# Attention after a GeGLU gate on one core: when the tiles of a burst are finished, and when the last output weights are loaded

## The chip, the cores and the metric

The kernel runs on one core of one Trainium2 chip. Its time is the device time of one execution in microseconds; the figure for a kernel is the median over its runs. The engines are named as in the profile: PE (TensorE) for matmuls and PEld for its weight loads, DVE (VectorE), ACT (ScalarE), POOL (GpSimd), SP (SyncE). POOL and SP issue transfers here; an issue takes its place in the queue of the engine that issues it.

## The reference

All arrays are bf16. `x` is 2048 x 448, 16 query heads share 8 heads of keys and values, a head has 256 columns, and the last 512 cached keys are attended.

```python
xn = _layernorm(x)
q = (xn @ wq)                       # 448 x 4096, 16 heads
scores = einsum("bhqd,bhkd->bhqk", q, k[last 512]) * 256 ** -0.5
s = (softmax(scores) @ v) @ wo      # wo is 4096 x 448
g = _silu((_gelu(xn @ w_gate) * (xn @ w_up)) @ w_down)
return x + s * g
```

## The kernel before

The 2048 rows are 16 tiles of 128, in 4 chunks of 512. First comes the feed-forward part over all chunks; it writes the gate `g` to `g_all` in DRAM. Then comes attention: 64 steps `m` (`NS`, loop at L895), 16 heads for each chunk. A step issues `s_mm(m)` (L712): for each of four tiles two score matmuls into a bank of the set AB, an exponential on ACT into `p` (three slots, L720), and for each pair of tiles one reciprocal and two scalings on DVE into `pn` (three slots of a pair each, L724, L727) and one DMA transpose `pT<-pn` on SP. Then the step issues `pv(m - 2)` (L733): eight matmuls of `va` with `pT` into two banks of the set BB, which ACT and DVE evacuate into `oTh` (`oT` in the last chunk). The lag of two steps is `LAG`.

The queries `qT` are made ahead of the heads, in groups (`groups`, L346): a query group at m = 18, 34, 50 makes eight heads, in four calls of `q_group` (L694) of two heads each, and so do those at 26 and 42; the one at 58 makes six. A call runs matmuls of `xnT` with `wq` and evacuates four banks: three on ACT and one on DVE (L707) where `end` is true, two and two elsewhere.

The first three chunks are not multiplied by `wo` in the plain way. At m = 17, 33, 49 `burst` (L798) multiplies `oTh` and sums of it by prepared weights `wt` and `w3` and leaves the chunk's projection transposed, in four blocks of rows. These are transposed back by DMA transposes on SP: `sN` early in the burst, three `sT` near its end. Then `burst_end(c, t4)` (L874) finishes one of the chunk's four tiles: three DVE multiplications of `sT` and `sN` with the gate tile `g` into `tmpb`, and in `wo_end` (L756) one addition onto the row tile `xr`. `wo_end` also issues three transfers on POOL: the load of the gate tile two tiles ahead (`g` has two slots), the store of the finished tile to `out`, and the load of the row tile three tiles ahead (`xr` has three slots), which must wait until the store has read the slot. "The first, second and third end" are the ends of chunks 0, 1 and 2, in the query groups at m = 18, 34 and 50 (`end`, L898).

The last chunk is multiplied by `wo` itself after the 64 steps (L930 to L944). The tile `wo` lies where `wt` and `w3` lay, so it can be loaded once the third burst's products have read those. Before, its four quarters of 896 KB are issued on POOL right after the third burst's call (L922 to L926), ahead of the query group at m = 50.

All engines run their instructions in the order of these calls. `Plan` (L43) derives the waits: an instruction waits by semaphore for those whose data or slots it needs, and an engine stands still until the wait is over. A call of `dma` on POOL is no exception: a waiting load holds the issues behind it.

Of the kernel before, what the change touches and what calls it, by code (L numbers as in the profile page):

```python
# [12 lines left out]
P = 128  # L13
# [155 lines left out]
def bass_recurrent_scan__sliding_block_cached__geglu_ffn__prompt_kernel(  # L169
# [15 lines left out]
    Hq = HD // Dh  # L185
# [7 lines left out]
    NCO = HD // P  # L193
# [17 lines left out]
    with es:  # L211
# [3 lines left out]
        def place(name, shape, dt, at=None):  # L215
            size = {BF16: 2, F16: 2, F32: 4}[dt]
            for n in shape[1:]:
                size *= n
            size = (size + 31) // 32 * 32
            if at is None:  # L220
                at = base[0]
                base[0] += size
            assert at + size <= nc.sbuf_usable_end, (name, at + size, nc.sbuf_usable_end)
            return nc.alloc_sbuf_tensor_at(name, list(shape), dt, offset=at), at, at + size

        def sbuf_bufs(at, size, n):
            return [K.buf(at + i * size, size) for i in range(n)]
# [56 lines left out]
        wo, _, _ = place("wo", [P, NCO, D], BF16, at=rw)  # L284
        b_wo = sbuf_bufs(rw, 8 * D * 2, NCO // 8)
# [67 lines left out]
        def dma(q, o, i, reads=(), writes=()):  # L353
            K.op(q, lambda e, o=o, i=i: e.dma_start(o, i), reads, writes, dma=True)  # L354
# [4 lines left out]
        def act(o, i, func, reads, writes, scale=1.0):  # L359
            K.op("act", lambda e, o=o, i=i: e.activation(o, i, func, scale=scale), reads, writes)  # L360

        def add(eng, o, x, y, reads, writes, op=ALU.add):
            K.op(eng, lambda e: e.tensor_tensor(o, x, y, op), reads, writes)  # L363

        def mms(lst, reads, writes, after=()):
            def fn(e):
                ins = None
                for (o, l, r, st, sp) in lst:
                    ins = e.matmul(o, lhsT=l, rhs=r, start=st, stop=sp, skip_group_check=True)  # L369
                return ins  # L370
            return K.op("pe", fn, reads, writes, after=after)
# [156 lines left out]
        def bk(pairs, j):  # L528
            return pairs[j // 2] + j % 2
# [8 lines left out]
        def down(c, pairs):  # L538
            for t4 in range(4):
                t = c * 4 + t4  # L540
                b = bk(pairs, t4)
                mms([(bank[b][:, 0:D], actT[:, c % 2, f, t4 * P:(t4 + 1) * P], wd[:, f, :], f == 0, f == NF - 1)
                     for f in range(NF)], [b_wd] + b_actT[c % 2], (b_ps[b],))
                s = t % 2
                act(tmp[:, s, 0:D], bank[b][:, 0:D], ACT.Tanh, (b_ps[b],), b_tmp[s], scale=0.5)
                K.op("dve", lambda e, t=t, b=b, s=s: e.scalar_tensor_tensor(
                    out=g2w[:, t % 4, :], in0=tmp[:, s, 0:D], scalar=1.0, in1=bank[b][:, 0:D],
                    op0=ALU.add, op1=ALU.mult), b_tmp[s] + [b_ps[b]], (b_g2w[t % 4],))
                dma("sp", g2d[t], g2w[:, t % 4, :], (b_g2w[t % 4],), (b_g2d[t],))
# [144 lines left out]
        def q_group(n, pairs, more_act=False):  # L694

            c, h = divmod(n, Hq)
            units = [(b, lambda j, k, i=i: wq[:, k, (h + i) * Dh + j * P:(h + i) * Dh + (j + 1) * P],
                      wqr[:, h + i, :], slice(c * QC, (c + 1) * QC), b_wql[h // HG][:1], b_wql[h // HG][1:], b_xnT[c * 4:c * 4 + 4])
                     for i, b in enumerate(pairs)]
            group(units, 0, QC, True, True)  # L700
            for i, b in enumerate(pairs):
                s = qs(n + i)
                act(qT[:, s, 0, :], bank[b], ACT.Copy, (b_ps[b],), (b_qT[s][0],))
                if more_act and i:
                    act(qT[:, s, 1, :], bank[b + 1], ACT.Copy, (b_ps[b + 1],), (b_qT[s][1],))
                    continue
                K.op("dve", lambda v, s=s, b=b: v.tensor_copy(qT[:, s, 1, :], bank[b + 1]),  # L707
                     (b_ps[b + 1],), (b_qT[s][1],))
# [24 lines left out]
        def pv(m):  # L733
            h = m % Hq
            g, x = h // 2, m % NPT
            for e in range(2):
                b = BB[m % 2 * 2 + e]
                mms([(bank[b].rearrange("p (t q) -> p t q", q=P), va[:, g, j, e * P:(e + 1) * P],
                      pT[:, x, :, :, j, :].rearrange("p a t q -> p (a t) q"), j == 0, j == NJ - 1)
                     for j in range(NJ)], [b_va[g]] + b_pT[x], (b_ps[b],))  # L740
                i = 2 * h + e
                o, f = (oTh, WS) if m < NS - Hq else (oT, 1.0)
                if e == 0:
                    act(o[:, i, :], bank[b], ACT.Copy, (b_ps[b],), (b_oT[i],), scale=f)
                else:
                    K.op("dve", lambda v, i=i, b=b, o=o, f=f: v.tensor_scalar(  # L746
                        o[:, i, :], bank[b], f, None, op0=ALU.mult), (b_ps[b],), (b_oT[i],))
# [8 lines left out]
        def wo_end(t, c0, c1, mult, bt, y):  # L756

            x, g = t % NXR, t % NG2
            bx = [b_xr[x][i] for i in range(2) if (c0 < CUT, c1 > CUT)[i]]
            mult(g2[:, g, :], b_g2[g])  # L760
            if t + NG2 < NT and c1 == D:
                load_g2(t + NG2)
            add("dve", xr[:, x, c0:c1], y[:, c0:c1], xr[:, x, c0:c1], bt + bx, bx)
            dma("sp" if t >= NT - 4 else "pool", out_view[:, t, c0:c1], xr[:, x, c0:c1], bx, ())
            if t + NXR < NT and c1 == D:
                dma("pool", xr[:, x, :], x_view[:, t + NXR, :], (), b_xr[x])
# [107 lines left out]
        def burst_end(c, t4):  # L874
            t = c * 4 + t4
            s, u = t % 2, t4 // 2
            y = tmpb[:, s, 0:D]

            def mult(g, bg):
                two = lambda x, lo, hi: x[:, 0:2 * N2].rearrange("p (n d) -> p n d", n=2)[:, :, lo:hi]  # L880
                for at, i, reads in ((lambda x: two(x, 0, P), sT[:, t4, 0:2, :], b_sT[:2]),
                                     (lambda x: two(x, P, N2), sT[:, t4, 2, :].rearrange("p (n d) -> p n d", n=2), b_sT[2:]),
                                     (lambda x: x[:, 2 * N2:D], sN[:, t4 % 2, u * R:u * R + R], [b_sN])):
                    add("dve", at(y), i, at(g), reads + [bg], b_tmp[s], ALU.mult)
            wo_end(t, 0, D, mult, b_tmp[s], y)

        LAG = 2
        late = []
        NS = NQC * Hq

        act(tmp[:, 1, 0:1], nhalf[:, :], ACT.Exp, (b_nhalf,), (b_tmp[1][0],))
# [2 lines left out]
        BB.extend(bk(nxt, j) for j in range(4))  # L894
        for m in range(NS):  # L895
            if m in groups:
                for i in range(m, groups[groups.index(m) + 1], 2):
                    end = m > Hq and m % Hq == LAG  # L898
                    q_group(i, (cur, nxt)[((i - m) // 2 + (m == Q0 + QS)) % 2], end)
                    for t4 in {4: (0, 1), 6: (2, 3)}.get(i - m, ()) if end else ():  # L900
                        burst_end(m // Hq - 1, t4)
                if m == 0:
                    K.reuse([b for x in b_pT for b in x] + b_pn + b_p32)
            if m > Hq and m % Hq == LAG:
                K.reuse(b_pn + b_p32)
            s_mm(m)
            if m < LAG:
                down(NQC - LAG + m, nxt)
                if m == LAG - 1:
                    K.reuse(b_oT + [b for y in b_qT[:QS - Q0] for b in y])  # L910
                    assert not CASTS and not SUMS
                    K.reuse(b_sT + [b_sN])
                    for t in range(NG2):
                        load_g2(t)
            if len(late) == LAG:
                pv(late.pop(0))
            if m > Hq and m % Hq == LAG - 1:
                if m // Hq == 1:
                    for b in b_xs:
                        b.old.extend(y for t in range(4) for z in b_xnT[t] for y in z.readers + [z.writer])  # L920
                burst(m // Hq - 1)
                if m // Hq == NQC - 1:  # L922
                    K.reuse(b_wo)
                    for i in range(NCO // 8):
                        dma("pool", wo[:, i * 8:(i + 1) * 8, :],
                            A_wo.rearrange("(c p) d -> p c d", p=P)[:, i * 8:(i + 1) * 8, :], (), (b_wo[i],))  # L926
            late.append(m)
        c = NQC - 1
        LATE = NCO - 2 * (LAG + 1)
# [70 lines left out]
```

The softmax here doesn't subtract the row's maximum and nothing guards it: scores larger than these inputs give would overflow.

## Time and profile before

| what | value |
|---|---|
| runs | 569.97, 562.45, 565.86, 563.88 us |
| median of the four | 564.87 us |
| profiled execution | 569.97 us, of it the span of the profile 568.2 us |
| mean granted clock of PE | 0.988 |
| PE busy | 549.0 us, 97% of the span |
| burst of chunk 0, 1, 2 ends, query group begins | 244.07, 353.36, 457.98 us |
| query group ends, heads begin | 256.50, 365.78, 470.41 us |
| issue of wo's quarters | 451.15, 458.36, 459.24, 460.11 us; to landing 5.9, 7.6, 10.5, 12.2 us |

The page is one execution. Its first section gives each engine's busy time, its second the span in slices, the fourth the chain that ended last, the fifth groups of instructions with what ended the idle time before them. Beside it the trace can be asked for the busy time in any stretch, for the instructions in order of time, and for the transfers. In a timeline line stand the start, the time, the engine, the line of the code, the operation, the tiles written and read, the shape and how many alike; in square brackets the idle time of the engine before it and what ended that. Matmuls have the line of a helper, L369, additions and multiplications of two tensors L363, plain ACT copies L360 and plain transfers L354.

### The profile page before, as it was taken

Reading aid. Unit: us, or ns where it says so; the run is one execution under the profiler, and the core shown is the slowest. Engines: PE = TensorE matmul, PEld = TensorE weight load, DVE = VectorE, ACT = ScalarE, POOL = GpSimd, SP = SyncE. Lnnn points to the kernel's source line nnn. Section 1 sums busy time; section 2 is a strip of 40 time slices with the busy share of each in tenths; the row PEclk is TensorE's granted clock in tenths of the full one; section 3 lists DMA queues with packets and bytes.
Section 4 is the critical chain, followed back from the end, with each engine's and each line's share of the span. In section 5 each row is a group of like instructions: output and inputs, shape, how many; then the busy total and the mean of one; then the engine's idle time right before and its main releaser. Section 6 shows DMA issues by size and latency. Waiting matters only on the chain.

```text
span 568.2 us, 11445 instructions
## 1 busy us (share of the span) xinstructions
PE 549.0 (97%) x4419; PEld 289.0 (51%) x4444; DVE 346.9 (61%) x804; ACT 309.9 (55%) x783; POOL 44.1 (8%) x83
## 2 busy tenths in 40 slices
PE   9999999999999999998799999989999995999997
PEld 5554444445444446953344489434446952444455
DVE  6664645753557668746565795377478734675722
ACT  5334446653568576057566831677586054776700
POOL 1141500000000000003000000120000013100000
PEclk9999999999999999999799999999999999899999
DMA  9665499712316548027642840387087174972711
GB/s 292 131 184 120 103 299 265 113 46 78 92 38 148 112 87 137 8 33 129 150 112 55 150 99 10 60 178 158 20 149 150 40 183 148 164 155 57 144 24 58
DMA packets 177766, 66.46 MB, mean 117 GB/s; under 512 B 159856, under 2 KB 173680, under 8 KB 177712
## 3 DMA queue, kind: packets, MB, share of 16 engines
q1 hardware_dynamic: 172960, 52.76, 44.2%
q0 software_dynamic: 3984, 12.39, 8.1%
q8 instruction: 35, 0.57, 0.5%
q10 hardware_dynamic: 768, 0.57, 0.3%
q14 instruction: 19, 0.16, 0.1%
HBM read 23.43 MB, written 3.67 MB: 48 GB/s over the span
## 4 chain that ended last, share of the span: by engine, by line
PE 81%; DMA 9%; DVE 5%; ACT 3%; issue 2%; POOL 1%; ACTq 0%; DVEq 0%
PE bank L369 80%; DMA pT<-pn 4%; DVE pn L727 3%; ACT p L720 3%; DMA sT<-xnT 2%; DMA g<-g_all 1%; DMA out_dram<-xr 1%; PE bank L486 1%; DVE rden L724 1%; DVE tmpb L363 0%; DVE oTh L746 0%; POOL g L354 0%; POOL xr L354 0%; DVE xr L363 0%; ACT qT L360 0%
## 5 line engine op out<-in xcount | busy, mean ns | idle before, releaser
L720 ACT ACTIVATE p<-bank 128x512 f32<-128x512 f32 x256 | 150.6, 596 | 43.3 <-DVE pn L727 32.9
L369 PE MATMUL bank<-pT,va 128*128 128x512 bf16 x512 | 124.5, 387 | 5.6 <-DMA pT<-pn 3.5
L369 PE MATMUL bank<-kT,qT 128*128 128x512 bf16 x487 | 120.9, 385 | 9.0 <-ACT p L720 6.7
L727 DVE TENSOR_SCALAR pn<-p,rden 128x512 bf16<-128x512 f32 x256 | 113.2, 485 | 12.0 <-DMA pT<-pn 7.7
L369 PE MATMUL bank<-xnT,wq 64*128 64x512 bf16 x768 | 94.9, 376 | 0.5 <-DVE oTh L746 0.5
L369 PEld LDWEIGHTS bank<-kT,qT 128*128 128x128 bf16 x512 | 49.8, 99 | 71.7 <-ACT p L720 8.4
L369 PEld LDWEIGHTS bank<-pT,va 128*128 128x128 bf16 x512 | 50.2, 99 | 70.0 <-DMA pT<-pn 7.0
L369 PE MATMUL bank<-xnT,wgu 64*128 64x512 bf16 (+2 forms) x768 | 83.9, 350 | 0.1
L360 ACT ACTIVATE qT<-bank 128x512 bf16<-128x512 f32 x76 | 44.1, 596 | 54.1 <-PE bank L369 52.5
L707 DVE CAST qT<-bank 128x512 bf16<-128x512 f32 x52 | 35.1, 692 | 46.9 <-PE bank L369 46.8
L369 PEld LDWEIGHTS bank<-xnT,wq 64*128 64x128 bf16 x768 | 36.6, 94 | 47.1 <-ACT p L720 1.7
L369 PEld LDWEIGHTS bank<-xnT,wgu 64*128 64x128 bf16 x768 | 37.0, 94 | 36.9 <-issue 0.7
L535 DVE TENSOR_TENSOR actT<-bank,gl 128x512 bf16<-128x512 f32 x56 | 37.8, 690 | 26.5 <-PE bank L369 19.9
L360 ACT ACTIVATE gl<-bank 128x512 bf16<-128x512 f32 x56 | 33.2, 597 | 37.1 <-PE bank L369 34.9
L720 ACT ACTIVATION_READ_ACCUMULATOR p<-bank 128x1 f32 x256 | 51.4, 201 | 0.0
L724 DVE RECIPROCAL rden<-rsum 128x2 f32<-128x2 f32 x128 | 21.2, 165 | 47.3 <-ACT p L720 47.2
L369 PE MATMUL bank<-wd,actT 128*128 128x448 bf16 x224 | 43.0, 353 | 0.0
L354 POOL DMA_DIRECT2D g<-g_all x16 | 8.8, 549 | 351.8 <-DVE tmpb L363 287.6
L746 DVE TENSOR_SCALAR oTh<-bank 128x512 f16<-128x512 f32 x48 | 32.8, 684 | 0.8 <-PE bank L369 0.8
L369 PEld LDWEIGHTS bank<-wd,actT 128*128 128x128 bf16 x224 | 21.8, 98 | 21.0 <-DVE mv L419 0.4
L369 PE MATMUL bank<-sr,wt 128*64 128x256 f16 x576 | 31.9, 273 | 0.0
L369 PEld LDWEIGHTS bank<-sr,wt 128*64 128x64 f16 x576 | 31.5, 110 | 0.0
(63 smaller groups left out, 415.3 us busy)
## 6 DMA issues: line engine op xcount, KB each, us to landing
wo<-in_A_wo_dram POOLq DMA_DIRECT2D x4, 896.0 KB, 9.0
wtb<-in_A_wo_dram POOLq DMA_DIRECT2D x4, 768.0 KB, 7.4
wq<-in_A_wq_dram SPq DMA_DIRECT2D x2, 1536.0 KB, 8.3
va<-in_A_v_cache_dram SPq DMA_DIRECT2D x8, 256.0 KB, 6.1
pT<-pn SPq DMA_TRANSPOSE x128, 2.8
g_all<-g2w SPq DMA_DIRECT2D x16, 112.0 KB, 2.1
xr<-in_A_x_dram POOLq DMA_DIRECT2D x16, 112.0 KB, 2.6
g<-g_all POOLq DMA_DIRECT2D x16, 112.0 KB, 2.5
```

Source lines behind the costliest of these rows:

```text
L354: K.op(q, lambda e, o=o, i=i: e.dma_start(o, i), reads, writes, dma=True)
L360: K.op("act", lambda e, o=o, i=i: e.activation(o, i, func, scale=scale), reads, writes)
L369: ins = e.matmul(o, lhsT=l, rhs=r, start=st, stop=sp, skip_group_check=True)
L486: ins = e.matmul(bank[b][:, 0:w], lhsT=gl[:, 0, 0:P], rhs=gl[:, 0, 0:w], start=True, stop=True)
L535: K.op("dve", lambda e: e.tensor_tensor(actT[:, c % 2, f, :], bank[b + 1], gl[:, s, :], ALU.mult), (b_ps[b + 1], b_gl[s]), (b_actT[c % 2][ ...
L707: K.op("dve", lambda v, s=s, b=b: v.tensor_copy(qT[:, s, 1, :], bank[b + 1]), (b_ps[b + 1],), (b_qT[s][1],))
L720: K.op("act", lambda e, b=b, r=r, z=z: e.activation(p32[:, z, :], bank[b], ACT.Exp, scale=att_scale, accum_out=rsum[:, r:r + 1]), (b_ps[b] ...
L724: K.op("dve", lambda e, r=r: e.reciprocal(rden[:, r - 1:r + 1], rsum[:, r - 1:r + 1]), b_rsum[r - 1:r + 1], b_rden[r - 1:r + 1])
L727: K.op("dve", lambda e, r=r - 1 + t, z=(n - 1 + t) % NP32, y=y, t=t: e.tensor_scalar(pn[:, y, t, :], p32[:, z, :], rden[:, r:r + 1], None, ...
L746: K.op("dve", lambda v, i=i, b=b, o=o, f=f: v.tensor_scalar(o[:, i, :], bank[b], f, None, op0=ALU.mult), (b_ps[b],), (b_oT[i],))
```

## The change

In an end's query group the tiles are finished one at a time: tile 0 after the second call of `q_group`, tile 1 after the third, tile 2 after the fourth. Before, tiles 0 and 1 followed the third call and tiles 2 and 3 the fourth. Tile 3 now follows in the step after (m = 19, 35, 51), behind that step's `pv`.

The four loads of `wo` leave the burst. A new `load_wo` issues the next quarter on POOL, with the same source, destination and queue. It is called in the loops of the last two query groups: at m = 50 behind tile 1's and behind tile 2's end, at m = 58 after the first and the second call of `q_group`. On POOL this gives the order: g, out, xr of tile 0; g, out, xr of tile 1; wo; g, out, xr of tile 2; wo; g, out, xr of tile 3; wo, wo.

```diff
+        to_load = list(range(NCO // 8))
+
+        def load_wo():
+            i = to_load.pop(0)
+            dma("pool", wo[:, i * 8:(i + 1) * 8, :],
+                A_wo.rearrange("(c p) d -> p c d", p=P)[:, i * 8:(i + 1) * 8, :], (), (b_wo[i],))
+
...
                     q_group(i, (cur, nxt)[((i - m) // 2 + (m == Q0 + QS)) % 2], end)
-                    for t4 in {4: (0, 1), 6: (2, 3)}.get(i - m, ()) if end else ():
-                        burst_end(m // Hq - 1, t4)
+                    if end and i > m:
+                        burst_end(m // Hq - 1, (i - m) // 2 - 1)
+                    if m >= NS - Hq + LAG and (end and i - m > 2 or not end and i - m < 4):
+                        load_wo()
...
             if len(late) == LAG:
                 pv(late.pop(0))
+            if m > Hq and m % Hq == LAG + 1:
+                burst_end(m // Hq - 1, 3)
             if m > Hq and m % Hq == LAG - 1:
...
                 burst(m // Hq - 1)
                 if m // Hq == NQC - 1:
                     K.reuse(b_wo)
-                    for i in range(NCO // 8):
-                        dma("pool", wo[:, i * 8:(i + 1) * 8, :],
-                            A_wo.rearrange("(c p) d -> p c d", p=P)[:, i * 8:(i + 1) * 8, :], (), (b_wo[i],))
             late.append(m)
```

## The prediction

> **What bounds the kernel now.** The page first, then busy time cut at the stages that the change touches, then the timeline inside two of them, then the transfers. By the page TensorE (PE) is busy nearly throughout:
>
> ```profile
> PE 549.0 (97%) x4419; PEld 289.0 (51%) x4444; DVE 346.9 (61%) x804; ACT 309.9 (55%) x783; POOL 44.1 (8%) x83
> ```
>
> So only PE's idle or slow microseconds can be won. The windows show where they are: the eight heads after a query group. Three such stretches follow a burst's end (rows 1, 2, 4), row 3 follows a group without one. Columns: time, busy PE, PEld, DVE, ACT, POOL, granted clock, DMA share, GB/s.
>
> ```profile
> 256.50:291.55 35.05, 30.81 (x127) 12.87 (x130) 21.82 (x61) 24.92 (x74) 5.39 (x10) 0.90 0.70 138
> 365.78:395.93 30.15, 28.15 (x127) 12.07 (x130) 21.51 (x61) 24.86 (x74) 5.52 (x10) 1.00 0.75 161
> 303.90:331.48 27.58, 27.47 (x127) 12.38 (x130) 20.57 (x54) 24.29 (x73) 0.00 (x0) 1.00 0.67 134
> 470.41:507.49 37.08, 30.85 (x127) 12.88 (x130) 23.93 (x69) 24.86 (x74) 6.47 (x12) 0.91 0.71 149
> ```
>
> 27.58 is what eight heads take when PE never waits. The ends cost 7.47, 2.57 and 9.50 us above it. The first two begin alike; the first end's timeline:
>
> ```profile
> 252.71 0.69 DVE L707 CAST qT<-bank 128x512 bf16<-128x512 f32 x1 [2.33 <-PE bank L369]
> 257.61 0.54 POOL L354 DMA_DIRECT2D g<-g_all  x1
> 260.12 0.43 DVE L363 TENSOR_TENSOR tmpb<-sT,g 128x256 bf16<-128x256 bf16 x2 [2.65 <-DMA g<-g_all]
> 261.70 0.60 ACT L720 ACTIVATE p<-bank 128x512 f32<-128x512 f32 x1 [2.38 <-DVE pn L727]
> 262.45 0.60 PE L369 MATMUL bank<-kT,qT 128*128 128x512 bf16 x2 [1.26 <-ACT p L720]
> 272.90 2.31 PE L369 MATMUL bank<-pT,va 128*128 128x512 bf16 x5 [2.88 <-DMA pT<-pn]
> ```
>
> The fourth tile's end waits in DVE's queue for its g; head 18's pn stands behind it, then ACT, then PE (1.26). The 2.88 later is a late pT transpose, and half clock follows. The third end differs:
>
> ```profile
> 458.36 2.63 POOL L354 DMA_DIRECT2D wo<-in_A_wo_dram  x3 [6.31 <-PE bank L369]
> 472.50 0.23 DVE L363 TENSOR_TENSOR tmpb<-sT,g 128x128 bf16<-128x128 bf16 x1 [4.99 <-DMA sT<-xnT]
> 474.78 1.04 PE L369 MATMUL bank<-pT,va 128*128 128x512 bf16 x4 [1.84 <-DVE qT L707]
> 481.26 1.03 PE L369 MATMUL bank<-kT,qT 128*128 128x512 bf16 x2 [4.15 <-ACT p L720]
> ```
>
> The wo load delays the sT transpose (12.63 us from issue to landing; 2.4 to 4.0 in the other ends), and DVE holds a qT evacuation and the pn behind it. How transfers share the engines, first while wo and sT both move, then in steady heads:
>
> ```profile
> q0 software_dynamic: 278, 1.14, 94.2%
> q1 hardware_dynamic: 285, 0.07, 9.7%
> ...
> q1 hardware_dynamic: 4224, 1.05, 67.4%
> ```
>
> In 468.1 to 471.4 the queues gave packets one for one: 278 of wo (4.1 KB) against 285 of sT (256 B). The second row is four pT transposes, 1056 packets each or 66 per DMA engine. A quarter of wo has some 219 packets, 14 per engine. So a transpose that meets a quarter moves 14 of its 66 packets until the quarter is through.
>
> **The change part by part.** The sum is against the profiled execution's 569.97 us, the slowest of the four runs, 5.10 above the median; its span is 568.2, and the 1.8 around it stays.
>
> 1. Tiles' ends earlier. Each is four DVE instructions (0.28 + 0.15 + 0.18 + 0.39, some 0.95 us) and three transfers on POOL's queue (g, out, xr). The first three move ahead by one qT evacuation each, into DVE's 2.33 us waits: cost nothing. Without that cover an evacuation is up to 0.95 late. The first needs sT: landed at 249.96 in the first end, against 250.38 when DVE gets there, 0.42 to spare. The third tile needs g, asked for at about 251.1 and 2.4 under way, so there by 253.5; DVE reaches it at 256.42. The 2.65 wait goes, and pn starts when ACT's second exponential is read, near 258.8, not 261.19. Next late would be out and xr, each waiting 2.1 for the out before it on POOL; nothing near needs them.
>
> 2. The fourth tile one head later. Its 0.95 sits in DVE ahead of head 20's (36's, 52's) pn, and what queues behind is reciprocal, pn, the transpose on SP and PE's pv. In row 3 pT lands 1.45 ahead of pv (issued 308.17, 2.70 under way, pv at 312.32), and DVE is busy 20.57 of 27.58, so it regains the time. Its three transfers now fall among transposes, whose landing in the second end rose from 2.7 to 4.1 under such traffic. Bounds 0 and 0.9 us (0.95 + 1.4 less 1.45); I take 0.3, nearer to row 3, since the traffic is three transfers and then over. SP's order does not change.
>
> So end 1 falls from 7.47 to 0.3, -7.2, and end 2 from 2.57 to 0.3, -2.3. That the first end's late pT goes too is open: a run without it has only the second end's loss, and its gain is -2.3.
>
> 3. wo moved. Before, four POOL issues stood ahead of the third end's transfers and ran beside the query group, where PE needs no transposes. Now nothing but POOL's own order holds them: in the changed program's order they carry no wait. With the third end's clock (first end + 213.91): g, out, xr twice, each xr waiting for its out, puts quarter 1 at 471.9, when the query group is over. Its packets run 473.4 to 476.9. Quarter 2 follows the xr that waits for the out queued behind quarter 1: 479.3, packets to some 484.2. Quarters 3 and 4 follow the fourth tile's xr, near 486.7, back to back, long before the next group (507.5 before). The sT wait (4.99) and everything behind it goes, -9.5. But the quarters meet the pT transposes. With row 3's offsets from 470.41, each pv in turn moved by the waits before it:
> - head 50: second transpose issued 474.7, lands 479.4, wanted 478.8: 0.6 (0 to 1.3)
> - head 51: issued 478.2, stands until quarter 2 is through, lands near 485.2, wanted 482.9: 2.3 (1.0 to 3.3)
> - head 53: pn waits for head 51's buffer, so both transposes meet quarters 3 and 4 from 488.2. The pair takes 28 packets per engine: at 0.19 us (3.3 us, 278 / 16) 5.3, at the 0.28 of 460 to 471.8 (11.8 us, 672 / 16) 7.9. Landing 495.4 to 498, wanted 492.3: 4.5 (2.2 to 6.0)
> - clock: a window of 6.83 at 0.50 stands behind the 2.88 wait and another behind the 4.15, none behind 1.26:
>
> ```profile
> 272.03:278.86 6.83, 5.96 (x15) 2.10 (x16) 4.01 (x10) 3.80 (x11) 0.50 (x1) 0.50 0.81 164
> 480.25:487.07 6.82, 5.81 (x14) 2.09 (x15) 5.11 (x13) 4.50 (x13) 2.49 (x5) 0.50 0.89 210
> ```
>
> Half of the 5.9 busy is lost, 2.9. The 4.5 pays it surely, the 2.3 at one chance in six: 3.4 (0 to 5.8).
>
> With item 2's 0.3 that is 11.1, against 9.5: +1.6. Bounds: 0 + 0 + 1.0 + 2.2 + 0 = 3.2 and 0.9 + 1.3 + 3.3 + 6.0 + 5.8 = 17.3, so -6.3 and +7.8.
>
> [...]
>
> Sum: 569.97 - 7.2 - 2.3 + 1.6 = 562.1. From the median, if its first end is like the second: 564.87 - 2.3 - 2.3 + 1.6 = 561.9. I say 562.0.
>
> **The rivals.**
> - The quarters do not stop PE. For it: 1.45 of slack, and each quarter alone is short. Against: one packet for one, and two quarters back to back. The third end then costs its lower bound, 3.2, or 0.3: 564.87 - 4.6 - 6.3 = 554.0, down to 564.87 - 4.6 - 9.2 = 551.1. With part of the waits left I take 555.
> - It ends slower than before: the pair of quarters at the pace of 460 to 468, dead time included, holds head 53 for the full 6.0 and both long waits bring half clock. The third end costs its upper bound, 17.3: 564.87 - 4.6 + 7.8 = 568.1. It turns slower once that end costs over 9.5 + 4.6 = 14.1, and by over 1% at 19.7. For it: three quarters took 11.8 us. Against: the single quarter ran through in 3.4.
> - sT late for the earlier first tile: by over 0.42 it delays DVE, but the next evacuation is due at 252.71, so under 2 us costs nothing; 562 stays.
>
> **How the numbers follow.** Forecast (559.2 to 564.9) 0.50; quarters hidden (below 559.2) 0.32; slower than before 0.18, half of it beyond 1%, which takes a pair of quarters slower than any here; its pace is what I know least. A measurement can tell about 1%, 5.65 us. So faster 0.32, same 0.59, slower 0.09. Range: 555.0 (near the lower bound's 554.0) to 568.0 (the upper bound), about one in ten left out on either side. The likeliest case's own range is 559.2 to 564.9.
>
> **What would show it.** Right: in the third end no DVE wait on sT, PE waits on DMA pT<-pn at heads 50, 51 and 53, two wo issues adjacent near 487, pT landings of 5 to 9 us, half clock once. In ends 1 and 2 no DVE wait on g and eight heads in 28 us. Wrong: wo quarters 3 and 4 issued only in the next query group, pT landings under 4.2 in the third end, or new waits on DVE's reciprocal behind the fourth tile's end.

## The result, and the profile after

The changed kernel took 565.09 us (median of 45 runs, 561.90 to 572.21), the kernel before 565.64 (71 runs, 562.45 to 569.97). The ratio is 0.999, with a 95% interval of 0.9978 to 1.0003: no difference that the measurement can tell. The profiled execution took 563.63 us, its span 561.9.

That nothing moved in the sum hides two large moves. The eight heads behind each end in the profile after; columns as in the prediction: stretch, time, busy PE, PEld, DVE, ACT, POOL, granted clock, DMA share, GB/s.

```profile
256.90:285.00 28.10, 27.64 (x127) 12.30 (x130) 21.50 (x61) 24.63 (x74) 4.02 (x7) 1.00 0.76 161
359.23:388.49 29.26, 27.64 (x127) 12.31 (x130) 21.53 (x61) 24.77 (x74) 3.92 (x7) 1.00 0.77 155
462.93:501.15 38.22, 31.19 (x127) 12.97 (x130) 21.82 (x61) 25.14 (x74) 7.52 (x11) 0.91 0.94 214
```

The first end is near the 27.58 of eight plain heads, the second 1.7 above it. The third is longer than before, and its DMA share rose from 0.71 to 0.94. In the first end DVE no longer stops for a gate tile; the first and the third tile's end and the first `pn` in its timeline:

```profile
250.70 0.42 DVE L363 TENSOR_TENSOR tmpb<-sT,g 128x256 bf16<-128x256 bf16 x2
256.75 0.42 DVE L363 TENSOR_TENSOR tmpb<-sT,g 128x256 bf16<-128x256 bf16 x2
259.38 0.88 DVE L727 TENSOR_SCALAR pn<-p,rden 128x512 bf16<-128x512 f32 x2
```

None has a bracket, so none waited, and `pn` starts 2.5 us after the heads begin (256.90) where it started 4.7 after (261.19, from 256.50). In the third end the wait on `sT` is gone too. In its place stand these; the timeline of the third end after, with wo's issues on POOL and each wait of PE:

```profile
464.59 0.90 POOL L354 DMA_DIRECT2D wo<-in_A_wo_dram  x1
472.42 0.90 POOL L354 DMA_DIRECT2D wo<-in_A_wo_dram  x1
473.49 2.83 PE L369 MATMUL bank<-pT,va 128*128 128x512 bf16 x8 [1.98 <-DMA pT<-pn]
481.01 3.51 PE L369 MATMUL bank<-pT,va 128*128 128x512 bf16 x8 [2.21 <-DMA pT<-pn]
482.45 1.78 POOL L354 DMA_DIRECT2D wo<-in_A_wo_dram  x2
492.34 1.90 PE L369 MATMUL bank<-pT,va 128*128 128x512 bf16 x8 [2.56 <-DMA pT<-pn]
```

The quarters are issued among the heads, the last two back to back, 19 us before the group at m = 58 in whose loop they are called (501.08). PE waits for the transposes of heads 50, 51 and 53, the three that the prediction names. Half clock follows the first two waits; two windows of the profile after:

```profile
474.31:477.72 3.41, 3.19 (x9) 1.21 (x8) 2.94 (x11) 2.18 (x6) 1.29 (x2) 0.50 0.99 212
481.14:484.55 3.41, 3.41 (x9) 1.22 (x8) 0.97 (x3) 1.28 (x3) 2.31 (x3) 0.50 1.27 127
```

And the transfers, first between those two waits, then while quarters 3 and 4 move, from 486.5 to 490 (queue, packets, MB, share of 16 engines; after the dots the transposes issued in the first stretch and their median landing in us):

```profile
q0 software_dynamic: 298, 1.11, 60.7%
q1 hardware_dynamic: 1058, 0.26, 39.4%
...
pT<-pn SPq DMA_TRANSPOSE x3, 7.0
```

```profile
q0 software_dynamic: 320, 1.35, 104.2%
q1 hardware_dynamic: 43, 0.00, 0.9%
```

In the first stretch, 6.5 us, the transposes got 1058 packets, what one transpose has; in steady heads four transposes passed in 6.9 us. They did not share packet for packet. Where no transfer of POOL and no other `pT` was in flight, a transpose's packets began 1.2 us after its issue (1.17 to 1.19, eight of them in the profile after); the one issued at 473.99 got none until 477, while the queue of `wo` moved 110 packets from 474.5 to 477. Only from 477 to 478 was it one for one (66 against 62), and most of the 1058 passed when the quarter was nearly through. Beside the pair it was 43 against 320. The transpose issued first beside quarter 1 (466.32) got none from 467.5 to 469 either, against 118 of `wo`. So the transposes that met quarter 1 or quarter 2 under way stood until it was nearly through; why, the trace does not show.

### The profile page after: what moved, and what is told of

The parts are those of the page before. It is cut to its first block, busy times and chain, and to the rows that moved or that the text cites. A ratio compares the mean times of both kernels' runs of the same rounds, so it can differ in the third digit from the quotient of the medians.

```text
span 561.9 us, 11445 instructions
## 1 busy us (share of the span) xinstructions
PE 545.9 (97%) x4419; PEld 288.7 (51%) x4444; DVE 346.6 (62%) x804; ACT 309.9 (55%) x783; POOL 44.6 (8%) x83
## 4 chain that ended last, share of the span: by engine, by line
PE 85%; DMA 6%; DVE 4%; ACT 3%; issue 1%; ACTq 0%; DVEq 0%
PE bank L369 84%; DMA pT<-pn 6%; DVE pn L727 3%; ACT p L720 3%; PE bank L486 1%; DVE rden L724 1%; ACT qT L360 0%; DVE oTh L746 0%; PE bank L467 0%; DVE qT L707 0%; DVE tmpb L363 0%; DVE xr L363 0%; DVE tmp L777 0%; DVE gl L399 0%; ACTq L155 0%
## 5 line engine op out<-in xcount | busy, mean ns | idle before, releaser
L369 PE MATMUL bank<-kT,qT 128*128 128x512 bf16 x487 | 118.6, 381 | 2.6 <-ACT qT L360 1.4
## 6 DMA issues: line engine op xcount, KB each, us to landing
wq<-in_A_wq_dram SPq DMA_DIRECT2D x2, 1536.0 KB, 11.1
```

## The experiments

In the tables "third end" and the like mean the time of the eight heads behind it, cut as in the windows above.

**How much the two kernels vary.** Two more profiles of each kernel, unchanged.

The kernel before: 

> The kernel before once more, for its spread: the eight heads of the first end took 35.05 us in the first profile and 31.12 in the run with the old ends and the moved wo. Theory A (the late pT and half clock of that profile are rare): 30 to 31.5, 30 to 31, 37, time near 565.6. Theory B (they are usual): 35 in the first end again.

> As the run before it: theory A 30 to 31.5, 30 to 31 and 37 us for the eight heads of the three ends; theory B 35 in the first end.

The changed kernel: 

> The changed kernel once more: 28.1, 29.3 and 38.2 us for the eight heads of the three ends in its first profile, 563.6 us in all, 1.5 under its median. Theory A (the third end varies with how quarters 2, 3 and 4 fall on the transposes, and its usual cost is higher than in that profile): 28 to 28.5, 28.5 to 29.5, and 37 to 43 in the third, which then holds nearly all of the difference between the runs. Theory B (the first two ends vary as much): one of them over 30.

> As the run before it: theory A 28 to 28.5, 28.5 to 29.5, and 37 to 43 us in the third end; theory B one of the first two over 30.

| profile | us | first end | second | third | elsewhere (span less the three) |
|---|---|---|---|---|---|
| before, of the prediction | 569.97 | 35.05 | 30.15 | 37.08 | 465.9 |
| before, second | 563.51 | 30.68 | 30.15 | 35.17 | 465.7 |
| before, third | 566.07 | 31.58 | 30.12 | 36.76 | 465.8 |
| after | 563.63 | 28.10 | 29.26 | 38.22 | 466.3 |
| after, second | 567.43 | 28.06 | 28.65 | 42.56 | 466.4 |
| after, third | 564.35 | 28.19 | 29.07 | 38.54 | 466.8 |

A wait in the first end of the third profile of before and, below, the third end of the second one after:

```profile
272.42 1.90 PE L369 MATMUL bank<-pT,va 128*128 128x512 bf16 x8 [2.50 <-DMA pT<-pn]
```

```profile
462.37:504.93 42.56, 32.35 (x127) 13.07 (x130) 21.91 (x61) 25.12 (x74) 7.79 (x11) 0.88 0.90 192
```

Theory A holds for both kernels, with one difference: in the first end of before only the half clock was a matter of one run. The transpose of head 19 is late in all three, and PE waits for it 2.88, 1.56 and 2.50 us; without half clock the end takes 31. After the change the first two ends are steady, and the third end makes the runs differ.

**The two parts apart.** First the tiles' ends alone, with wo in the burst:

```diff
-                    if m >= NS - Hq + LAG and (end and i - m > 2 or not end and i - m < 4):
-                        load_wo()
...
                     K.reuse(b_wo)
+                    for i in range(NCO // 8):
+                        load_wo()
```

> The tiles' ends as in the changed kernel, the four quarters of wo back in the third burst. Theory A (late g costs PE about 2 us in each of the first two ends; wo among the heads costs 10.6 in the third): ends 1 and 2 stay at 0.5 to 1.7 us over eight plain heads. In the third end the first tile's end waits for sT from about 457 to 465 and holds the DVE evacuation behind it, 8 us instead of 5, but only one evacuation and two tiles stand behind it in place of three tiles, so pn starts some 3 us sooner than before: third end 5 to 7 over. Time 565.6 - 2 - 1 - 3.5 = 559, 0.988 of before. Theory B (in a usual run the ends' edit brings nothing, since the traffic it moves delays the transposes instead): only the third end's gain is left, 562, 0.994. Theory C (the earlier wait for sT stops PE longer, since the evacuation behind it frees a bank of the scores): third end 12 or more, 566 or more, 1.00 or above.

Measured: 558.33 us, ratio 0.9872 (0.9843 to 0.9900); the ends took 28.21, 28.91 and 34.46. Theory A, whose 559 and 0.988 were close. The third end in its timeline: the first tile's end waits for `sT`, a `qT` evacuation behind it holds PE, and much later a transpose is late.

```profile
463.37 0.23 DVE L363 TENSOR_TENSOR tmpb<-sT,g 128x128 bf16<-128x128 bf16 x1 [4.92 <-DMA sT<-xnT]
464.77 1.47 PE L369 MATMUL bank<-kT,qT 128*128 128x512 bf16 x6 [2.12 <-DVE qT L707]
482.78 2.54 PE L369 MATMUL bank<-pT,va 128*128 128x512 bf16 x8 [2.58 <-DMA pT<-pn]
```

Then wo alone, with the ends as before:

```diff
-                    if end and i > m:
-                        burst_end(m // Hq - 1, (i - m) // 2 - 1)
+                    for t4 in {4: (0, 1), 6: (2, 3)}.get(i - m, ()) if end else ():
+                        burst_end(m // Hq - 1, t4)
...
-            if m > Hq and m % Hq == LAG + 1:
-                burst_end(m // Hq - 1, 3)
```

> The four quarters issued as in the changed kernel, the tiles' ends as before. Theory A: ends 1 and 2 as before; in the third no wait on sT, but 1.3 us for the late g and some 10 us of late transposes and half clock, 11 to 12 over eight plain heads against 9.5 before: 565.6 + 2 = 567.6, 1.003 to 1.004. Theory B (moving wo alone is worth nothing either way): 565.6, 1.000. Theory C (wo out of the query group gains, and the ends' edit loses it again): under 563, 0.995 or below.

Measured: 578.82 us, ratio 1.0222 (1.0177 to 1.0267); 31.12, 30.98 and 42.73 in the profiled run, which at 572.93 was the fastest of its six. Theory A in direction, but the price was put far too low: nearly 14 us, not 2. With the old ends POOL reaches the quarters in another pattern, one and then three back to back:

```profile
472.18 0.92 POOL L354 DMA_DIRECT2D wo<-in_A_wo_dram  x1
481.90 3.60 PE L369 MATMUL bank<-pT,va 128*128 128x512 bf16 x8 [4.44 <-DMA pT<-pn]
486.80 2.90 POOL L354 DMA_DIRECT2D wo<-in_A_wo_dram  x3
499.57 3.59 PE L369 MATMUL bank<-pT,va 128*128 128x512 bf16 x8 [4.79 <-DMA pT<-pn]
```

So the ends alone are worth 6.7 us (565.07, its own runs of before, less 558.33), and moving wo on top of them takes all of it back.

**wo held where PE needs no transposes.** The ends as in the changed kernel; quarter 1 in the burst, quarter 2 behind the landing of the last `sT`, quarters 3 and 4 behind PE's first and second call in the group at m = 58 (the expectation names that a little too early).

```diff
-        def load_wo():
+        def load_wo(after=()):
...
-                    if m >= NS - Hq + LAG and (end and i - m > 2 or not end and i - m < 4):
-                        load_wo()
+                    if m >= NS - Hq + LAG and not end and i - m < 4:
+                        load_wo([o for o in K.ops if o.eng == "pe"][-1:])
...
                 burst(m // Hq - 1)
+                landed = K.ops[-1:]
                 if m // Hq == NQC - 1:
                     K.reuse(b_wo)
+                    load_wo()
+                    load_wo(landed)
```

> The tiles' ends as in the changed kernel; quarter 1 of wo in the third burst, quarter 2 held until the last sT has landed, quarters 3 and 4 held on POOL until PE has issued the heads before the query group at m = 58. Theory A: no quarter meets the third end's first transposes except the tail of quarter 2, third end 0.5 to 2 over eight plain heads in place of 10.6; the group at 58 covers 9 of the 7 to 8 us that the last two take: 565.1 - 9 = 556, 0.983 to 0.986 of before. Theory B (the third end loses anyway, by the fourth tile's transfers among the transposes and not by wo): 562 or more, 0.994 or above.

Measured: 554.38 us, ratio 0.9813 (0.9789 to 0.9837). Theory A. The third end and the held issues of this kernel:

```profile
462.06:493.48 31.42, 27.82 (x127) 12.22 (x130) 21.31 (x61) 24.70 (x74) 5.68 (x10) 1.00 0.81 155
```

```profile
455.81 0.89 POOL L893 DMA_DIRECT2D wo<-in_A_wo_dram  x1 [12.11 <-DMA sT<-xnT]
496.91 0.90 POOL L893 DMA_DIRECT2D wo<-in_A_wo_dram  x1 [20.46 <-PE bank L369]
```

POOL stands still for 20.46 us, and nobody needs it. No half clock is left among the heads. The third end still lost 3.8 us, more than the 0.5 to 2 expected, although quarter 2 had landed at 461.3, before its heads began; its largest wait is one of 2.77 on a transpose. Run again beside the last experiments: 

> The held quarters once more, beside the next kernel on the same chip. Theory A (the delay of the fourth tile's end by one head is worth nothing by itself): equal to the next one within 1.5 us, both 554 to 557. Theory B (the delay is worth 2 to 3 us): 554, and the next 556.5 or more.

Measured: 554.09 us, 0.9795 (0.9766 to 0.9823); 28.26, 28.64, 29.95 (the third end 2.4 over). This version beats both kernels by about 2%.

**Which quarters cost.** Only quarters 3 and 4 held, 1 and 2 as in the changed kernel:

```diff
+                    if m >= NS - Hq + LAG and end and i - m > 2:
+                        load_wo()
                     if m >= NS - Hq + LAG and not end and i - m < 4:
                         load_wo([o for o in K.ops if o.eng == "pe"][-1:])
...
-                    load_wo()
-                    load_wo(landed)
```

> The changed kernel with quarters 3 and 4 held until PE is through with the first and the second call of the query group at m = 58; quarters 1 and 2 as in the changed kernel, behind the second and the third tile's end. Theory A (each quarter that meets transposes costs PE 1 to 3 us, the pair 4 to 6 and half clock): the third end falls from 38 to 43 to some 33 to 36, time 558 to 561. Theory B (the pair is covered by the lead that the earlier waits leave): 563 or more, as the changed kernel.

Measured: 560.32 us, 0.9909 (0.9883 to 0.9934); third end 36.13, with waits on transposes of 1.40 and 3.50 and one half-clock window of 6.83. Theory A. The other way round, quarters 1 and 2 as in the held kernel, 3 and 4 without a hold:

```diff
-                        load_wo([o for o in K.ops if o.eng == "pe"][-1:])
+                        load_wo()
```

> Quarter 1 in the burst and quarter 2 held for sT, as in the held kernel, but quarters 3 and 4 on POOL without a hold, behind the fourth tile's xr, where the changed kernel has them. Theory A: the pair meets the transposes of two or three heads, PE waits 4 to 6 us and half clock adds 2 to 3: third end 36 to 40, time 560 to 564. Theory B (a pair alone is covered): 555 to 557.

Measured: 562.31 us, 0.9952 (0.9926 to 0.9979); third end 41.75 in a run of 566.45. Theory A, with a larger wait than said:

```profile
480.12 1.91 POOL L893 DMA_DIRECT2D wo<-in_A_wo_dram  x2
493.76 3.31 PE L369 MATMUL bank<-pT,va 128*128 128x512 bf16 x8 [10.01 <-DMA pT<-pn]
```

Against the 554.1 to 554.4 of the held kernel, the first two quarters among the heads cost 6 us and the pair 8; both together, in the changed kernel, 11. They are less than additive; that a wait gives the later transposes a lead would explain it, but no run shows that by itself.

**The ends as before, wo held.** The held kernel with the old ends (the second diff above):

> The tiles' ends as before, the quarters held. Theory A (both parts count, each for itself): 31, 30 and 30 to 33 us for the eight heads of the three ends, 465.8 elsewhere and 1.8 around the span: 559 to 561, 0.990 to 0.993 of before. Theory B (the place of wo is all that counts, and the old ends lose only by chance): 29, 29 and 31, 556 or less.

Measured: 558.94 us, 0.9904 (0.9868 to 0.9939); 30.24, 29.92 and 30.51. Theory A: both parts count by themselves, wo's place 6.3 us (565.23 less 558.94) and the ends, on top of it, 4.6 (558.94 less 554.38).

**The fourth tile one head later.** The changed kernel with the fourth tile's end directly behind the third's:

```diff
                         burst_end(m // Hq - 1, (i - m) // 2 - 1)
+                        if i - m == 6:
+                            burst_end(m // Hq - 1, 3)
...
-            if m > Hq and m % Hq == LAG + 1:
-                burst_end(m // Hq - 1, 3)
```

> The changed kernel with the fourth tile's end directly behind the third's, not one head later; wo as in the changed kernel. Theory A: the fourth waits for its g, asked for behind the out and xr of the first tile at about 254.5 (in the first end) and there at 257.0, when DVE is through with the third tile: little wait, 0 to 0.5 us, so the delay by one head is worth at most 0.5 in each end and the ends one by one alone remove the wait: 565.1 to 566, 0.999 to 1.001. Theory B (the delay by a head is what removes the wait): a wait on g of 1 us or more in ends 1 and 2, 1 us in PE for each, 567 or more, 1.003.

Measured: 570.84 us, 1.0090 (1.0055 to 1.0125). Neither theory: the first two ends took 28.11 and 28.50 without a wait on g, as theory A said, and the time rose all the same. The fourth tile's transfers also stand between wo's quarters on POOL, and with them earlier the last three quarters went out together:

```profile
476.34 2.89 POOL L354 DMA_DIRECT2D wo<-in_A_wo_dram  x3
492.82 3.60 PE L369 MATMUL bank<-pT,va 128*128 128x512 bf16 x8 [12.51 <-DMA pT<-pn]
```

So this kernel measures three quarters together (third end 45.54, mean granted clock 0.85 in it, which is half clock for some 13.7 us) and not the delay. The same edit in the held kernel:

> The held quarters with the fourth tile's end directly behind the third's. Theory A (once each tile's g is asked for one evacuation earlier, the delay by one head is worth nothing): eight heads of the ends in 28.1, 28.5 and 30 to 31.5 us, time 553.5 to 555, the same as with the delay. Theory B (the delay pays): 29 to 30 in each end, 557 to 559.

Measured: 556.61 us, 0.9851 (0.9819 to 0.9884), between the theories and on another chip than the held kernel. Beside it on one chip, the run of the held kernel above with its 554.09 and this:

> The held quarters with the fourth tile's end directly behind the third's, once more. Theory A: as the run before it, within 1.5 us, 554 to 557. Theory B: 2 to 3 us slower than the run before it, 556.5 to 557.5.

Measured: 555.94 us, 0.9836 (0.9804 to 0.9868). The intervals of the ratios overlap, but every run of the kernel with the delay (553.74 to 554.26) was below every run without (555.25 to 558.04). And the edit in the kernel with the ends alone:

> The ends one by one with the fourth directly behind the third, wo in the burst as before. Theory A: as the run with the ends alone, 557.5 to 559.5, 0.986 to 0.989 of before. Theory B (the delay is worth 2 to 3 us): 560.5 to 562, 0.991 to 0.995; with it in the third end, where the fourth tile's g stands behind wo, DVE waits for g.

Measured: 561.50 us, 0.9924 (0.9897 to 0.9952), against 558.33 with the delay. Theory B, if a little low for the first pair: the delay is worth 1.9 us with wo held and 3.2 with the ends alone. It is not the wait on g in ends 1 and 2, which is absent there either way; in the third end of the last kernel, where g stands behind wo, DVE does wait 2.5 us for it, as theory B said. What differs in every pair is head 18's second transpose: it landed after 3.3 to 3.4 us with the delay and after 4.07 to 6.93 without, beside the fourth tile's transfers. In the two profiles without the delay and with wo held (4.28 and 5.91) PE waited 0.6 and 2.2 us for it, in the last kernel (6.93) 3.2, with half clock. That this is the whole difference is not shown: between the two held kernels run side by side the second end differs most (28.64 and 29.49).

## Why the prediction was wrong, and where it was right

It named 562.0 and the range 555 to 568, in which 565.09 lies; but the range spans 13 us and has no change at all well inside it, and the gain of half a per cent that it forecast is not there. What gains and what loses at each end was named rightly. The sizes were not: the first end gained more than said, and the other three terms missed by more than that to the other side. Against the mean of the profiles in the table (for the first end before, the two usual ones):

| term | predicted | measured |
|---|---|---|
| first end, from a usual run | -2.3 | 28.12 - 31.13 = -3.0 |
| second end | -2.3 | 28.99 - 30.14 = -1.15 |
| third end | +1.6 | 39.77 - 36.34 = +3.4 |
| elsewhere | 0 | 466.5 - 465.8 = +0.7 |
| sum | -3.0 | -0.1 |

The medians of all runs differ by -0.55.

- *Item 1*, the tiles' ends earlier: right. DVE reached the first tile's end at 250.70, the last `sT` had landed at 250.30 (issue 246.34, 3.96 under way); no wait. The text left open whether the first end's late `pT` goes too, and took the second end's 2.3 for a run without it. It is usual (waits of 1.56 and 2.50 in the other two profiles of before), and it went: head 19's second transpose landed after 4.9 to 6.2 us before and 4.4 after, and PE waited at most 0.36. So a usual first end gained 3.0. Why it lands sooner was not separated.
- *Item 2*, 0.3 us for the fourth tile among the heads: nearly held in the first end (28.1, 0.5 over), too low in the second, which lost 1.4. There head 36's transposes landed after 4.7 and 5.0 us, and PE waited 1.5; the 1.45 of lead did not cover it. Two things met: the fourth tile's transfers and a packet of 16 KB in the instruction queue (below). In the four kernels without the delay the second of those transposes landed after 3.7 to 4.0.
- *Item 3*, wo among the heads, is the step that failed: +1.6 was forecast for the third end and +3.4 measured, 0.7 of the miss in its base and 1.1 in its cost. The 9.5 that the third end lost before came from the slowest of the four runs; the other two profiles lost 7.6 and 9.2, the mean is 8.8. The 11.1 after was met in two profiles (10.6 and 11.0) and missed in the third (15.0), the mean is 12.2. Within the first profile the waits were 2.0, 2.2 and 2.6 against 0.6, 2.3 and 4.5 predicted, the clock 3.3 (half of 3.19 and of 3.41) against 3.4. The first wait was longer: quarter 1 took 6.36 to land, and head 50's second transpose was issued 0.6 later after the heads began than reckoned and landed after 5.58 in place of 4.7. The last was shorter: what came before it had moved the `pv` of head 53 by 5 us and the landing by 3. Half clock came twice, not once.
- *The clock.* Forecast 3.4, measured 3.3. Half clock came behind waits of 1.98 and 2.21 us; the forecast had given the 2.3 one chance in six and the 4.5 certainty. It lasted 3.41 us at a time here, 6.83 in the profile before, and 10.24 in the run with quarters 1 and 2 held: once, twice and three times 3.413. The length of a wait did not decide alone: the 2.56 here and the 2.77 in the held kernel brought none. Where the wait fell went with it in the two profiles before and after. The starts of half clock lie 208.22 us apart before (272.03 and 480.25) and 6.83 after (474.31 and 481.14), 61 and 2 times 3.413. If the attention of each (165 to 535 us) is cut from such a start into stretches of 3.413, the four behind which half clock began hold 2.08 and 3.13 us without a matmul before and 1.98 and 2.21 after, and no other stretch at full clock holds more than 1.60. The wait of 2.56 is cut into 1.60 and 0.96. These are four cases, and they do not show why the clock falls.
- *The rivals.* That the quarters stop nobody is refuted by the 3.5 and 10.01 us that PE waited where only some of them were left. The dear case is nearly what the second profile after shows, 15.0 against its 17.3, but not by a slower pair: quarters 3 and 4 landed after 6.67 and 8.35 us there and after 6.74 and 8.25 in the first. The waits were 2.0, 3.6 and 4.3, with half clock for 3.41 and 6.83. Where three quarters go out together the kernel is slower than before (1.009, 1.022). The late `sT` did not come.
- *One packet for one*, the rate on which item 3 reckons, was right for sT before (278 against 285) and wrong for most of the time in which `pT` meets a quarter (none against 110, 43 against 320). It cost the forecast little, since at either rate most of a transpose's packets are left for the quarter's end: 14 packets of 0.018 us, the median of the 256 B packets in both profiles, are 0.25 us. Why the rates differ is not shown. What the meeting costs the held kernel shows, in which the two queues are kept apart: 11 us.
- *Elsewhere* was put at nothing and measured +0.7. Most of it is not the change's: the heads that began at 201.52 to 201.57 in the three profiles before began at 201.90 to 202.22 in the three after, ahead of the first instruction that the change moves.

## What to carry to other kernels

A call's place in the program is not a time: quarters 3 and 4, which waited for nothing of their own, went out right behind the `xr` load ahead of them on POOL, at 482.45, 19 us before the group in whose loop they are written. A load that should run beside a certain stretch needs a dependency that holds it there, at a queue that nobody needs meanwhile; the held kernel lets POOL stand for 20.46 us and takes 554. Beside transposes in packets of 256 B the plain load in packets of 4 KB took almost all of the engines (104.2% against 0.9% from 486.5 to 490), so put such a load where nothing waits for a transpose, and above all not two or three in a row: the pair cost 8 us, and both kernels with three in a row were slower than before (1.009, 1.022). Waits of 1.98 and 2.21 us were followed by half clock and waits of 2.56 and 2.77 were not, so the length of a stall alone does not tell its price. Before a stall is priced from one profile, look where that execution lies among the runs: here one stretch of it was 4 us above its usual time, and the base of the decisive term was 0.7 us above the mean of three.

## What the runs showed of the hardware that was not expected

Away from wo and the ends a `pT` transpose lands after 2.7 us, but now and then after 4 to 5, at nearly the same heads in the profiles before and after (9, 12, 17, 28, 33, 44, 49 and 62 in both; 52, in the third end, before alone). Counting only transposes with no POOL transfer in flight, all 19 that took over 4 us in these two profiles met a packet of 16 KB in the instruction queue. The 31 that met such a packet landed after 4.29 us in the median before and 4.17 after, and the 147 that met no packet of the instruction queues after 2.73, none above 2.90. Such a packet took 1.16 us in the median before and 1.06 after, one of a transpose 0.018. The moment of head 36 in the profile after:

```profile
q8 instruction: 1, 0.02, 1.7%
...
pT<-pn SPq DMA_TRANSPOSE x3, 4.7
```

This is a coincidence counted over 19 cases; no run moved such a packet by itself, and since the heads are nearly the same each time, something else at those places is not ruled out.
